# Attention and a two-layer feed-forward on one NeuronCore: three quarters of the first layer as seven products, and kv in 64-column tiles

## The chip, the core and the metric

The kernel runs on one core of a Trainium2 chip. The metric is the device time of one execution in microseconds (us). "TensorE" multiplies matrices into PSUM; VectorE (DVE in the profile), ScalarE (ACT) and GpSimd (POOL) work beside it; SyncE (SP), GpSimd and ScalarE issue DMAs. A 128x512 float32 result in PSUM is one bank in this text.

## The reference

```python
kv = einsum('bhsd,bhse->bhde', k, v)            # batch 8, 8 heads, sequence 576, head 64
o  = einsum('bhsd,bhde->bhse', q, kv)
o  = o / sqrt(mean(o*o, -1) + 1e-6) * g_norm
x  = o.transpose(0, 2, 1, 3).reshape(4608, 512)
h  = x @ w_in                                   # 512 x 2048
g  = h * sigmoid(1.702 * h)
out = g @ w_out                                 # 2048 x 512
```

All inputs and the output are float32; the kernel casts to float16 on the way in and accumulates in float32.

## The kernel before

The 4608 tokens are nine tiles of 512: tiles t = 0 to 7 hold the first 512 tokens of batch element t, and tile 8 the eight remainders of 64. A tile has two stages. The **hidden stage** forms h transposed, 16 columns of 128 hidden units by 512 tokens, each gated by ScalarE into `gT`. The **projection** multiplies `gT` by `w_out`. Attention for the next batch element is woven into both: kv of t+1 in the hidden stage, its q·kv rows, norms and the transpose of x in the projection. The order of each engine's instructions is the order in which the program issues them (a manual schedule). `dense` runs a tile, and the lists `u1` and `u2` (filled with `at1(step, ...)` and `at2(step, ...)`) say after which step of the hidden stage or of the projection an attention piece is issued.

From tile 2 on (`SEVEN`) part of the hidden stage, and from tile 1 on the whole projection, use Strassen's scheme in its Winograd form: a product of matrices cut into quarters takes seven products of quarters in place of eight, for sums of the inputs and outputs formed on VectorE.

- In the hidden stage (`hid_seven`), `PARTS = (2, 6)` names two groups, each of two column blocks and the two that lie `HF` = 8 blocks higher: eight of 16 columns. A product is four matmuls of 256 columns (`SevenIn.product`). The other eight columns are plain: four matmuls of 512 columns each, run as two halves. Products and halves alternate; a group's seven go in the order 1, 5, 6, 2, 7, 3, 4.
- Products 1, 6, 7 and 4 of a group accumulate one after the other in one PSUM bank (x), 5 and 3 in another (z), and 2 has its own (y). So what a product leaves has to be read before the next one writes into its bank: ScalarE copies 1 (L548) and 6 (L552), VectorE copies 5 (L550) and adds 2, 7 and 3 (L557), ScalarE gates the four results (L525).
- The sums of the weights are formed once (`w_in_sum`, L478), the sums of x once a tile (`Sums.form`, L492), the sums of `gT` (`Seven.sums`, L588) as its columns become ready.
- The projection (`Seven.run`, L656) is seven products of 16 matmuls of 256 columns.

kv of tiles 2 to 7: the rows of k and v are loaded 64 partitions a head, so that the two heads of a pair fill 128 (`load_half`, L112). VectorE packs k into `kpad`, each head in its own 64 of 128 columns beside zeros (`pack_k`, L224), and a pair of heads takes nine matmuls of 64 columns on the full array (`kv`, L233). The four pairs lie at four steps of the hidden stage. Four copies on VectorE (`keep_kv`, L249) place the results. The next loads of k wait for the packing, those of v for the kv matmuls. Batch element 0 is computed otherwise (`First`): 96 partitions, six rows each, and 64-column matmuls for each head (L393).

Of the kernel before, what the change touches and what calls it, by code (L numbers as in the profile page):

```python
# [7 lines left out]
F16 = mybir.dt.float16  # L8
# [4 lines left out]
P = 128  # L13
# [3 lines left out]
def kernel(  # L17
# [29 lines left out]
    PH = P // 2  # L47
    NH = S // PH
    assert PH == D and PH * NH == S

# [16 lines left out]
    kpad = const.tile([P, NPAIR, NH, P], F16)  # L67
# [15 lines left out]
    PARTS = (2, 6)  # L83
# [26 lines left out]
    def load_half(n, b, c0, c1):  # L110
        for l in range(2):
            nc.gpsimd.dma_start(  # L112
                out=raw[n][l * PH : (l + 1) * PH, c0:c1, 0 : NH * D],
                in_=srcs[n][b].rearrange("(c l) (p j) d -> l p c (j d)", l=2, j=NH)[l][:, c0:c1],
            )

    def load_kv(b):
        load_half("k", b, 0, NPAIR)
        load_half("v", b, 0, NPAIR)
# [86 lines left out]
    class Attention:  # L206
# [14 lines left out]
        def pack_k(self, c0=0, c1=NPAIR):  # L221
            for l in range(2):
                r = slice(l * PH, (l + 1) * PH)
                nc.vector.tensor_copy(  # L224
                    out=kpad[r, c0:c1, :, l * D : (l + 1) * D],
                    in_=kraw[r, c0:c1, 0 : NH * D].rearrange("p c (j d) -> p c j d", j=NH),
                )

        def kv(self, c):
            if c % self.KEEP == 0:  # L230
                self.kvp = ps_a.tile([P, NPAIR, D], F32, name="kvp", tag="att")
            for j in range(NH):
                nc.tensor.matmul(  # L233
                    self.kvp[:, c, :],
                    kpad[:, c, j, :],
                    vbuf[:, c, j * D : (j + 1) * D],
                    start=(j == 0),
                    stop=(j == NH - 1),
                )
            if (c + 1) % self.KEEP == 0:  # L240
                self.keep_kv(c + 1 - self.KEEP, c + 1)

        def keep_kv(self, c0, c1):
            kb = self.kb.rearrange("p (c l) e -> p c l e", l=2)
            for half in range(2):
                to = slice(half * D, (half + 1) * D)
                for hl in range(2):
                    r = slice(hl * D, (hl + 1) * D)
                    nc.vector.tensor_copy(kb[to, c0:c1, hl, to], self.kvp[r, c0:c1, :])  # L249
# [133 lines left out]
    class First(Early):  # L383
# [4 lines left out]
        def kv(self, c):  # L388
            t = ps_o.tile([P, D], F32, name="kv0", tag="o")
            for j in range(NJ):  # L390
                for hl in range(2):
                    x = slice((hl * NJ + j) * D, (hl * NJ + j + 1) * D)
                    nc.tensor.matmul(  # L393
                        t[hl * D : (hl + 1) * D, :],
                        kraw[0:PE_, c, x],
                        vbuf[0:PE_, c, x],
                        start=(j == 0),
                        stop=(j == NJ - 1),
                    )
# [66 lines left out]
    def w_in_sum(n):  # L466
        for g, i in enumerate(PARTS):
            a11, a12, a21, a22 = quarters(
                w_in_sb, slice(i * P, (i + 2) * P), slice(0, KH)
            )  # L470
            o = [ws[:, m, :, 2 * g * P : 2 * (g + 1) * P] for m in range(4)]
            op, a, b = (
                (nc.vector.tensor_add, a21, a22),
                (nc.vector.tensor_sub, o[0], a11),
                (nc.vector.tensor_sub, a11, a21),
                (nc.vector.tensor_sub, a12, o[1]),
            )[n]
            op(o[n], a, b)  # L478
# [15 lines left out]
    class SevenIn:  # L494


        ORDER = (1, 5, 6, 2, 7, 3, 4)

        def __init__(self, hid, xs, g):
# [4 lines left out]
            self.both = s12  # L504
# [24 lines left out]
        def product(self, p):  # L529
# [23 lines left out]
            elif p == 4:  # L553
                self.gate(1, 0, o)
            else:
                which, r, n = {2: ("s1", 0, 0), 7: ("s5", 1, 1), 3: ("s2", 0, 1)}[p]
                nc.vector.tensor_add(s[which], o, s[which])  # L557
                self.gate(r, n, s[which])
# [132 lines left out]
    def hid_seven(t, hid, seven, units1):  # L691

        pairs = [i for i in range(HF) if all(i not in (g, g + 1) for g in PARTS)]
        halves = [(f, k) for i in pairs for f in (i, HF + i) for k in (0, KH)]
        xs = xsums.pop(t)
        steps = [halves[0], halves[1]]
        for g in range(len(PARTS)):
            part = SevenIn(hid, xs, g)
            for n, p in enumerate(part.ORDER):
                steps += [(part, p), halves[2 + g * len(part.ORDER) + n]]  # L700
        for n, (f, k) in enumerate(steps):
            if isinstance(f, SevenIn):
                f.product(k)
            else:
                for ko in (k, k + 1):
                    hid.mm(ko, f)
                if k:
                    hid.gate(f)
            for u in units1.get(n, ()):
                u()  # L710
            which = {17: 0, 20: 1, 23: 2, 26: 3}.get(n)
            if which is not None:
                seven.sums(0, 4, (which,))
        seven.sums(4, 8, (0,))

    def dense(t, units1, units2, group, deep, hid=None):
# [52 lines left out]
        else:  # L769
            i = 4 if t >= SEVEN else 6  # L770
# [100 lines left out]
    load_half("k", 1, 0, 2)  # L871
    load_w_out(8, 10)
    load_w_out(10, 12)
    load_half("v", 1, 0, 2)
    load_half("k", 1, 2, NPAIR)
    load_half("v", 1, 2, NPAIR)
# [4 lines left out]
    SEVEN = 2  # L881
    HALVED = (2, 3, 4, 5, 6)
# [9 lines left out]
    for t in range(NT):  # L892
# [12 lines left out]
        if t == 0:  # L905
# [6 lines left out]
            for l in range(2):  # L912
                r = slice(l * PH, (l + 1) * PH)
                at1(8, nc.vector.memset, kpad[r, :, :, (1 - l) * D : (2 - l) * D], 0.0)
                at1(9, nc.vector.memset, kvd[l], 0.0)
            at1(13, load_q, 2)
            for c in range(NPAIR):
                at1(12, of(1, "pack_q", c))
                at2(9 + 3 * c, of(1, "q", c))
                if c % 2 == 0:  # L920
                    at2((21, 0, 38)[c], of(1, "pack_k", c, c + 2))
# [7 lines left out]
        elif b < B:  # L929
            if t == 1:  # L930
# [10 lines left out]
                for n, at in ((2, 82), (0, 86), (1, 92), (3, 97)):  # L941
                    at2(at, w_in_sum, n)
            f0 = 5 if t == 1 else 3
            late = 14 if t == 1 else 15
            if t == 1:
                at1(f0, start, b)
# [53 lines left out]
```

## Time and profile before

| | us |
|---|---|
| three executions | 275.87, 275.74, 274.12 (median 275.74) |
| the profiled execution | 274.47 |
| its span, first to last instruction | 272.7 |

In the profile's groups a row gives line, engine, operation, tiles and shapes, the count, then busy time in us and the mean in ns, then the idle time before and what ended it. In the timeline a row begins with start and duration in us; merged rows (x4) last from the first's start to the last's end. In the rows of stretches, each engine has its busy time and number of instructions, in the order PE, weight loads, DVE, ACT, POOL; then TensorE's granted clock, the DMA share and GB/s. A matmul's row lasts until its result is in PSUM; the next one starts long before.

### The profile page before, as it was taken

To read this page: it belongs to the slowest core of one execution; us is meant where nothing else is said; L and a number is where in the kernel's file an instruction comes from. 1 tells how busy PE (TensorE), PEld (TensorE's weight loads), DVE (VectorE), ACT (ScalarE), POOL (GpSimd) and SP (SyncE) were. 2 spreads that over 40 slices of the span, in tenths; PEclk is the share of its full clock that TensorE was granted. 3 is DMA by queue.
4 is the path that set the end of the run, shared out by engine and by line. 5 is a ranking of instruction groups with operands and counts; after the bars stand their busy time and mean duration, and the time that the engine had idled before them with its cause. 6 is when DMAs were issued, how large, how long until landed. Compare 5 with 4: busy or idle time off the path is not lost.

```text
span 272.7 us, 5717 instructions
## 1 busy us (share of the span) xinstructions
PE 263.0 (96%) x2328; PEld 189.3 (69%) x2328; DVE 184.7 (68%) x331; ACT 172.8 (63%) x309; POOL 50.3 (18%) x82
## 2 busy tenths in 40 slices
PE   7799999999999999999999999999999999999993
PEld 6344554458767787778777877788778867876782
DVE  1642454958998787779777976797689646455731
ACT  3578509858857865686577657775678477228610
POOL 8772363114014101410031003200000000000000
PEclk9999999999999999999999999999999999999999
DMA  8999999989989929993899289937500610021005
GB/s 175 182 199 204 205 203 199 270 161 155 132 161 166 141 46 185 180 164 31 185 174 181 33 177 170 189 36 170 153 0 2 155 77 2 0 99 58 0 2 154
DMA packets 56540, 35.29 MB, mean 129 GB/s; under 512 B 31810, under 2 KB 53826, under 8 KB 56386
## 3 DMA queue, kind: packets, MB, share of 16 engines
q0 software_dynamic: 25184, 17.91, 46.1%
q1 hardware_dynamic: 30848, 16.49, 26.3%
q10 hardware_dynamic: 482, 0.52, 0.6%
q8 instruction: 18, 0.29, 0.5%
q14 instruction: 8, 0.07, 0.1%
HBM read 36.70 MB, written 9.44 MB: 169 GB/s over the span
## 4 chain that ended last, share of the span: by engine, by line
PE 81%; DVE 7%; ACT 4%; DMA 3%; POOL 2%; issue 1%; DVEq 0%; ACTq 0%
PE o L656 30%; PE hT L449 26%; PE h L538 15%; PE o L750 4%; PE kvp L233 3%; DMA w_in_sb<-in_moe_w_in_dram 3%; PE outR L297 2%; DVE gS L588 2%; ACT gT L525 1%; DVE ws L478 1%; ACT gT L458 1%; PE ss L345 1%; DVE w_in_sb L204 1%; POOL qraw L93 1%; DVE x L325 1%
## 5 line engine op out<-in xcount | busy, mean ns | idle before, releaser
L449 PE MATMUL hT<-xT,w_in_sb 128*128 128x512 f16 x320 | 85.4, 379 | 1.3 <-DMA w_in_sb<-in_moe_w_in_dram 1.3
L458 ACT ACTIVATE gT<-hT 128x512 f16<-128x512 f32 x88 | 50.8, 601 | 12.5 <-PE hT L449 12.4
L656 PEld LDWEIGHTS <-gS 128*128 128x128 f16 x512 | 49.6, 98 | 6.7 <-DVE gS L588 0.9
L656 PE MATMUL o<-tw,gS 128*128 128x256 f16 x384 | 47.6, 273 | 0.3 <-DVE gS L588 0.3
L449 PEld LDWEIGHTS <-w_in_sb 128*128 128x128 f16 x352 | 32.5, 98 | 19.3 <-DMA w_in_sb<-in_moe_w_in_dram 1.6
L656 PEld LDWEIGHTS <-gT 128*128 128x128 f16 x384 | 37.0, 98 | 5.7
L525 ACT ACTIVATE gT<-qf 128x512 f16<-128x512 f32 x42 | 26.4, 629 | 18.7 <-DVE qf L557 18.5
L557 DVE TENSOR_TENSOR qf<-h,qf 128x512 f32<-128x512 f32 x42 | 28.3, 688 | 9.9 <-PE h L538 9.6
L656 PE MATMUL o<-w_out_sb,gT 128*128 128x256 f16 x256 | 33.7, 273 | 0.0
L538 PEld LDWEIGHTS <-ws 128*128 128x128 f16 x224 | 21.9, 98 | 14.8 <-issue 0.3
L588 DVE TENSOR_TENSOR gS<-gT 128x1024 f16<-128x1024 f16 (+1 forms) x34 | 22.3, 656 | 13.8 <-ACT gT L458 13.7
L112 POOL DMA_DIRECT2D kraw<-in_k_dram x16 | 9.9, 622 | 88.6 <-DVE kpad L224 82.6
L538 PE MATMUL h<-xS,ws 128*128 128x256 f16 x168 | 25.2, 272 | 0.1
L538 PEld LDWEIGHTS <-w_in_sb 128*128 128x128 f16 x168 | 16.4, 98 | 11.9 <-issue 1.9
L633 DVE TENSOR_TENSOR osb<-o,qf 128x512 f32<-128x512 f32 (+1 forms) x25 | 16.6, 665 | 11.6 <-issue 6.4
L347 ACT ACTIVATE ln<-ss,eps_t 128x512 f32<-128x512 f32 (+1 forms) x16 | 9.3, 582 | 15.0 <-PE ss L345 14.9
L625 ACT COPY qf<-o 128x512 f32<-128x512 f32 (+1 forms) x26 | 14.5, 560 | 5.4 <-PE o L656 5.4
L750 PE MATMUL o<-w_out_sb,gT 128*128 128x512 f16 x64 | 16.7, 379 | 0.0
L325 DVE TENSOR_TENSOR x<-outR,sum 128x512 f16<-128x512 f32 x24 | 14.9, 684 | 1.0 <-ACT sum L321 1.0
L900 ACT ACT_TABLE_LOAD x12 | 15.4, 1283 | 0.2
L656 PE MATMUL o<-w_out_sb,gS 128*128 128x256 f16 x128 | 15.4, 273 | 0.0
L656 PE MATMUL o<-tw,gT 128*128 128x256 f16 x128 | 15.3, 272 | 0.0
(97 smaller groups left out, 348.1 us busy)
## 6 DMA issues: line engine op xcount, KB each, us to landing
out_dram<-osb SPq DMA_DIRECT2D x10, 512.0 KB, 3.0
kraw<-in_k_dram POOLq DMA_DIRECT2D x12, 288.0 KB, 6.3
vbuf<-in_v_dram POOLq DMA_DIRECT2D x12, 288.0 KB, 7.4
qraw<-in_q_dram POOLq DMA_DIRECT2D x3, 512.0 KB, 9.0
qbuf<-in_q_dram POOLq DMA_DIRECT2D x3, 512.0 KB, 9.7
out_dram<-osb SPq DMA_DIRECT2D x6, 192.0 KB, 5.2
w_in_sb<-in_moe_w_in_dram POOLq DMA_DIRECT2D x4, 256.0 KB, 7.9
w_out_sb<-in_moe_w_out_dram POOLq DMA_DIRECT2D x2, 512.0 KB, 13.9
```

The source lines that it names most:

```text
L325: nc.vector.tensor_mul(self.x16[:, j0 : j0 + 2, c0 : c0 + DM // 2].rearrange("p l (h d) -> p h l d", d=D), self.o[j][0].rearrange("p (h l ...
L449: nc.tensor.matmul(self.h[fo], w_in_sb[:, ko, fo * P : (fo + 1) * P], self.x[:, ko], start=(ko == 0), stop=(ko == KO - 1),)
L458: nc.scalar.activation(self.gT[:, fo, :], self.h[fo], AFT.Gelu_apprx_sigmoid)
L525: nc.scalar.activation(self.gT[:, to, n * TH : (n + 1) * TH], src, AFT.Gelu_apprx_sigmoid)
L538: nc.tensor.matmul(o[:, a], w, x, start=(p in (1, 2, 5) and a == 0 and k == 0), stop=(k == KH - 1), skip_group_check=True,)
L557: nc.vector.tensor_add(s[which], o, s[which])
L588: op(s[:, n, lo], a, b)
L625: nc.scalar.copy(self.kept[as_][:, m], ps)
L633: nc.vector.tensor_add(o, ps, self.kept[with_][:, m])
L656: nc.tensor.matmul(o, a, w, start=(p in (1, 2, 5) and i == 0 and (mo == 0 or split)), stop=(i == HF - 1), skip_group_check=True,)
L750: nc.tensor.matmul(os[mo], gT[:, fo, mo * P : (mo + 1) * P], w_out_sb[:, fo, :], start=(fo == 0), stop=(fo == FO - 1),)
L900: u2.setdefault(i, []).append(lambda: f(*args))
```

## The change

- `PARTS` becomes `(0, 3, 6)`: three groups, twelve of 16 columns as seven products (84 matmuls of 256 columns in place of 56), and four plain columns (16 matmuls of 512 in place of 32). Each group has its own copies, adds and gates, which makes 12 in place of 8 weight sums.
- The order of the steps is a list, `STEPS`. A group's products go 1, 2, 5, 6, 3, 7, 4, and the next group's 1 and 2 are placed between 7 and 4. Gates are issued one step later than what they gate. Between products 5 and 3, and between 7 and 4, two other steps now lie (in the second group kv stands between 5 and 3 as well).
- `READY` issues the sums of `gT` for columns 0 to 2 after steps 15, 18, 20 and 21, those for columns 3 and 4 after steps 24, 26, 28 and 29, and the first for columns 5 to 7 at the end. Before, they covered columns 0 to 3 and 4 to 7.
- kv runs as one block at the step "kv" (15), after step 11 in tile 1: for each of four pairs, six times two matmuls in 64-column tiles from 96 partitions, reading k as it was loaded. `kpad`, `pack_k`, `load_half` and the zeroing of `kpad` go. k and v are loaded in one DMA each, and both loads wait for kv's matmuls. Two of the four copies of kv go to ScalarE.
- Two of the four weight sums (`w_in_sum` 3 and 2, six instructions on VectorE) move from the projection of tile 1 to the first step of tile 2.

```diff
-    PARTS = (2, 6)
+    PARTS = (0, 3, 6)
...
     def load_kv(b):
-        load_half("k", b, 0, NPAIR)
-        load_half("v", b, 0, NPAIR)
+        early_load("k", b, 0, NPAIR)
+        early_load("v", b, 0, NPAIR)
...
+        def kv_product(self, t, c):
+            for j in range(NJ):
+                for hl in range(2):
+                    x = slice((hl * NJ + j) * D, (hl * NJ + j + 1) * D)
+                    nc.tensor.matmul(
+                        t[hl * D : (hl + 1) * D, :],
+                        kraw[0:PE_, c, x],
+                        vbuf[0:PE_, c, x],
+                        start=(j == 0),
+                        stop=(j == NJ - 1),
+                    )
...
-                    nc.vector.tensor_copy(kb[to, c0:c1, hl, to], self.kvp[r, c0:c1, :])
+                    copy = nc.scalar.copy if half else nc.vector.tensor_copy
+                    copy(kb[to, c0:c1, hl, to], self.kvp[r, c0:c1, :])
...
-                self.gate(1, 0, o)
+                return lambda: self.gate(1, 0, o)
...
-                self.gate(r, n, s[which])
+                return lambda: self.gate(r, n, s[which])
...
+        parts = [SevenIn(hid, xs, g) for g in range(len(PARTS))]
+        gates = []
+        for n, step in enumerate(STEPS):
+            behind, gates = gates, []
+            if step == "h":
+                f, k = next(halves)
                 for ko in (k, k + 1):
                     hid.mm(ko, f)
                 if k:
-                    hid.gate(f)
+                    gates.append(lambda f=f: hid.gate(f))
+            elif step != "kv":
+                g, p = step
+                gate = parts[g].product(p)
+                if gate:
+                    gates.append(gate)
+            for u in behind:
+                u()
             for u in units1.get(n, ()):
                 u()
-            which = {17: 0, 20: 1, 23: 2, 26: 3}.get(n)
-            if which is not None:
-                seven.sums(0, 4, (which,))
-        seven.sums(4, 8, (0,))
+            for i0, i1, which in READY.get(n, ()):
+                seven.sums(i0, i1, which)
+        for u in gates:
+            u()
+        seven.sums(5, 8, (0,))
...
+    STEPS = [(0, 1), (0, 2), "h", "h", (0, 5), (0, 6), "h", (0, 3), (0, 7), (1, 1), (1, 2), (0, 4)]
+    STEPS += ["h", (1, 5), (1, 6), "kv", (1, 3), (1, 7), (2, 1), (2, 2), (1, 4)]
+    STEPS += ["h", (2, 5), (2, 6), "h", (2, 3), (2, 7), "h", "h", (2, 4)]
+    KV = STEPS.index("kv")
+    READY = {n: [(0, 3, (w,))] for w, n in enumerate((15, 18, 20, 21))}
+    READY |= {n: [(3, 5, (w,))] for w, n in enumerate((24, 26, 28, 29))}
...
-                for n, at in ((2, 82), (0, 86), (1, 92), (3, 97)):
-                    at2(at, w_in_sum, n)
+                at2(82, w_in_sum, 0)
+                at2(90, w_in_sum, 1)
+            if t == 2:
+                at1(0, w_in_sum, 3)
+                at1(0, w_in_sum, 2)
...
-            at1(f0, of(b, "pack_k"))
-            for c in range(NPAIR):
-                at1(10 + c if t == 1 else 8 + 2 * c, of(b, "kv", c))
+            at1(late, of(b, "kv_all"))
```

More of the change, by code (lines that the diff above doesn't have):

```diff
@@ L219, in __init__ @@
                 self.x16 = attn.tile([P, J, DM], F16, name="x16", tag="x16", bufs=1)
[L221 to L227, printed above, removed]
         def kv(self, c):
@@ L389, in kv @@
             t = ps_o.tile([P, D], F32, name="kv0", tag="o")
[L390 to L399, printed above, removed]
+            self.kv_product(t, c)
             nc.vector.tensor_mul(
```

76 lines of the change are left out of this document (24 added, 52 removed).

## The prediction

> **What bounds the kernel now.** I read the page's shares first, then the stretches of one tile (its hidden stage, then its projection), then the timeline where TensorE pauses.
>
> ```profile
> span 272.7 us, 5717 instructions
> PE 263.0 (96%) x2328; PEld 189.3 (69%) x2328; DVE 184.7 (68%) x331; ACT 172.8 (63%) x309; POOL 50.3 (18%) x82
> ...
> 76.64:91.55 14.91, 14.57 (x127) 9.57 (x125) 13.59 (x26) 9.60 (x18) 4.63 (x7) 1.00 0.98 181
> ...
> 133.30:147.39 14.09, 14.07 (x125) 9.55 (x123) 11.96 (x22) 9.71 (x18) 4.62 (x7) 1.00 1.10 194
> ...
> 216.63:229.71 13.08, 13.08 (x90) 8.61 (x88) 8.17 (x14) 9.55 (x18) 0.00 (x0) 1.00 0.21 82
> ```
>
> TensorE is busy 96% of the span; in the hidden stage of tile 4 it is busy 14.07 of 14.09 us at full clock (1.00). That tile's first matmul is at 133.14 (below), so its stage is 14.25 us. But VectorE is busy 11.96 us of it and ScalarE 9.71, with 8.17 and 9.55 where there is no kv (tile 7). So TensorE bounds the kernel, and the other two are near enough to take over.
>
> ```profile
> 50.81 5.99 PE L449 MATMUL hT<-xT,w_in_sb 128*128 128x512 f16 x27
> ...
> 116.77 0.60 PE L538 MATMUL h<-xS,ws 128*128 128x256 f16 x4
> ...
> 117.95 1.28 DVE L557 TENSOR_TENSOR qf<-h,qf 128x512 f32<-128x512 f32 x2
> ...
> 118.69 0.60 PE L538 MATMUL h<-xS,w_in_sb 128*128 128x256 f16 x4
> ...
> 122.75 3.00 PE L656 MATMUL o<-tw,gS 128*128 128x256 f16 x26
> ...
> 133.14 1.03 PE L449 MATMUL hT<-xT,w_in_sb 128*128 128x512 f16 x4
> ```
>
> The only pause of such a stage is here: product 4 of the second group waits for the add that reads product 7 from the same PSUM bank. The first add runs 117.95 to 118.64, and TensorE goes on at 118.69, 0.05 later. A 512-column matmul costs (5.99-0.38)/26 = 0.216 us, a 256-column one (3.00-0.27)/25 = 0.109; a product (four) 0.436, a plain half (two) 0.432.
>
> **What TensorE saves.** Per tile from 2 to 8, 16 plain matmuls go (3.46 us) and 28 product matmuls come (3.05): -0.41.
>
> ```profile
> 7.25 0.38 PE L393 MATMUL kv<-vbuf,kraw 96*64 96x64 f16 x12
> ...
> 112.60 0.42 PE L233 MATMUL kvp<-vbuf,kpad 128*128 128x64 f16 x9
> 112.86 0.60 PE L449 MATMUL hT<-xT,w_in_sb 128*128 128x512 f16 x2
> ...
> 125.68 0.31 PE L268 MATMUL outT<-qTr,kvd 64*64 64x64 f16 x8
> 125.92 0.28 PE L656 MATMUL o<-tw,gS 128*128 128x256 f16 x1
> ```
>
> Now a pair's nine kv matmuls push the next matmul back 0.26, a tile's 1.04. The new kv is 48 matmuls in 64-column tiles. The row of 12 (six pairs) gives (0.38-0.20)/5.5 = 0.03 us for two. The 64x64 row shows the change of mode: the last matmul before it starts at 122.75+2.73 = 125.48, so the way in takes 0.20 instead of 0.11, and the way out 0.12. 24 pairs at 0.032 and both ways: 0.98, so -0.06 a tile. Bounds: 0.7 (no change of mode) to 1.3 (0.38 for each 12, less the tail). Tile 0's four separate kv pay the change each time: 0.09 in, 0.18 for twelve, 0.12 out, 0.39 against 0.26 now, +0.45 in all with rounding.
>
> [...]
>
> If nothing else changed, seven tiles would save 0.41 and six kv 0.06: -3.2 us.
>
> **What VectorE and ScalarE take on.** Mean durations by group (ns, after the bar), then rows of the timeline:
>
> ```profile
> L557 DVE TENSOR_TENSOR qf<-h,qf 128x512 f32<-128x512 f32 x42 | 28.3, 688 | 9.9 <-PE h L538 9.6
> L525 ACT ACTIVATE gT<-qf 128x512 f16<-128x512 f32 x42 | 26.4, 629 | 18.7 <-DVE qf L557 18.5
> ...
> L588 DVE TENSOR_TENSOR gS<-gT 128x1024 f16<-128x1024 f16 x30 | 20.6, 688 | 13.8 <-ACT gT L458 13.7
> ...
> L550 DVE COPY qf<-h 128x512 f32<-128x512 f32 x14 | 9.7, 692 | 3.9 <-PE h L538 3.5
> ...
> L552 ACT COPY qf<-h 128x512 f32<-128x512 f32 x14 | 8.2, 584 | 3.6 <-PE h L538 3.6
> ...
> L588 DVE TENSOR_TENSOR gS<-gT 128x512 f16<-128x512 f16 x4 | 1.7, 420 | 0.0
> ```
>
> ```profile
> 109.90 0.60 PE L538 MATMUL h<-xS,ws 128*128 128x256 f16 x4
> ...
> 110.60 0.69 DVE L557 TENSOR_TENSOR qf<-h,qf 128x512 f32<-128x512 f32 x1 [0.43 <-PE h L538]
> ...
> 113.07 1.73 DVE L249 CAST kvd<-kvp 64x256 f16<-64x256 f32 x4 [0.70 <-PE kvp L233]
> ...
> 115.03 0.60 PE L538 MATMUL h<-xS,ws 128*128 128x256 f16 x4
> ...
> 115.67 0.59 ACT L552 COPY qf<-h 128x512 f32<-128x512 f32 x1 [0.65 <-PE h L538]
> ...
> 121.17 1.10 ACT L305 ACTIVATE sq<-outR 128x512 f16<-128x512 f32 x2
> ```
>
> A product begun at 115.03 is copied from 115.67, one begun at 109.90 is added from 110.60: a result is taken 0.20 (copies) to 0.27 us after TensorE has moved on. In a queue the next instruction starts about 0.1 before the last one's end (two adds 1.28, two activations 1.10), so an add holds VectorE 0.60 and an activation ScalarE 0.48 to 0.53. The kv copies hold VectorE 0.43 each. A sum over three columns (768) lies between the 512 and 1024 rows: 0.555 (0.46 held), an estimate.
>
> The third group adds three adds and a copy on VectorE, two copies and the gating of four half-width results on ScalarE. Gone are packing k (two copies) and two of four kv copies from VectorE; the two go to ScalarE (estimate 0.38 each). By throughput both still fit into the stage. By order they do not. In the new order two steps (0.87 us) lie between products 5 and 3, and two between 7 and 4; the copy or add between needs 0.20+0.69+0.05 = 0.94 at once, and 0.12 to 0.8 more if something is queued in front. I therefore follow tile 4 by hand through the compiled order of the three queues (each instruction starts when its queue is free and its inputs are there), from the first matmul at 0. (g,p) is product p of group g; "3.11 for 3.04" is when TensorE can start that product, and when it would have without this wait. The input sums are done by 1.2:
>
> (0,3): copy of (0,5) 2.37 to 3.06, TensorE at 3.11 for 3.04. (0,7): ScalarE gates (0,2) and a plain column first, copies (0,6) 3.00 to 3.58; 3.63 for 3.55. (0,4): adds of (0,3) at 3.75, of (0,7) 4.35 to 5.04; 5.09 for 4.94. kv ends at 7.81. (1,7): ScalarE copies (1,1) to 5.59, VectorE adds (1,2) to 6.32, ScalarE then has three gates (6.36, 6.89, 7.37) ahead of the copy of (1,6), 7.84 to 8.43; 8.48 for 8.25. (1,4): VectorE has two kv copies from 7.92, a sum at 8.78, the add of (1,3) at 9.24 and then that of (1,7), 9.84 to 10.52; 10.57 for 9.78. (2,3): gate (1,3) 9.96, copy (2,1) to 11.08, add (2,2) 11.12, two sums, copy (2,5) 12.76 to 13.45; 13.50 for 12.75. (2,4): adds at 14.14 and 14.74 to 15.42; 15.47 for 15.24.
>
> The stage ends at 15.91 for 14.25: 2.31 us of waits, of which 1.5 are (1,4) and (2,3). Tiles 3 to 6: +1.65 each, +6.6. Tiles 7 and 8 have no kv; the same steps end at 15.15 for 13.08. A wait of 0.33 in their projection goes, as the last sums are now shorter:
>
> ```profile
> 231.46 0.60 PE L656 MATMUL o<-tw,gS 128*128 128x256 f16 x4
> 232.22 0.50 PE L656 MATMUL o<-tw,gS 128*128 128x256 f16 x3 [0.16 <-DVE gS L588]
> ```
>
> (232.22 follows 231.46+0.33 by 0.43 for 0.11.) So +1.75 each, +3.5. Tile 2 also gets six of the twelve weight sums (L478) after its first product, ahead of its first add:
>
> ```profile
> 74.85 1.42 DVE L478 TENSOR_TENSOR ws<-w_in_sb 128x512 f16<-128x512 f16 x4
> ...
> 76.64 0.81 PE L449 MATMUL hT<-xT,w_in_sb 128*128 128x512 f16 x3
> ...
> 77.46 0.76 DVE L478 TENSOR_TENSOR ws<-w_in_sb,ws 128x512 f16<-128x512 f16 x2
> 78.12 0.42 DVE L492 TENSOR_TENSOR xS<-xT 128x512 f16<-128x512 f16 x1
> ...
> 79.26 0.42 DVE L492 TENSOR_TENSOR xS<-xT,xS 128x512 f16<-128x512 f16 x1
> ```
>
> Its input sums, now where the two weight sums at 77.46 stood, end queueing at 78.93 (four in 1.14+0.33). Six weight sums at (1.42-0.42)/3 = 0.33 follow, so the first add starts at 80.94, 4.3 after the tile's start for 1.26. The copy of (0,5) then lets (0,3) go at 5.64, and (0,4) at 8.09 for 5.09. Its stage is 18.9 for 14.91: +4.0.
>
> Loads: k's (POOL) now waits for kv, as v's does, some 5 us later; one instruction replaces two. Its next use is a tile away. Nothing taken, bounds 0 to +1 a tile (rival below). Tile 1's kv: -0.06.
>
> Sum: 0.45 - 0.06 + 4.0 + 6.6 + 3.5 = +14.5 us on the profiled execution's 274.47 (span 272.7): 289.0. That execution is 1.3 below the median of 275.74.
>
> **Rivals.** (a) The interlocking hides the waits: -3.2, and the present pause of 0.19 and the 0.33 go: 270 to 272, faster. For it: VectorE's work fits the stage by throughput. It decides if the 2.6 us between the end of kv and the end of (1,7)'s add shrink under the 1.74 of four products. Against it: five measured durations in one queue. (b) Only waits with an idle queue remain: 0.07 at two places, 0.12 at three, 0.5 a tile, which the savings of 0.41, 0.06 and 0.19 cancel: 273 to 275, no difference. (c) Queues cost half of that, because an order or lag is a little kinder than followed: 278 to 283. (d) The later k load runs into the transposes of x.
>
> ```profile
> 107.85 1.40 POOL L112 DMA_DIRECT2D kraw<-in_k_dram  x2 [18.42 <-DVE kpad L224]
> ...
> 113.33 1.22 POOL L112 DMA_DIRECT2D vbuf<-in_v_dram  x2 [4.07 <-PE kvp L233]
> ...
> 133.16 0.42 DVE L492 TENSOR_TENSOR xS<-xT 128x512 f16<-128x512 f16 x1 [0.88 <-DMA xT<-x]
> ```
>
> k is asked for at 107.85 now, v at 113.33; afterwards both when kv ends. x of tile 4 lands at its very start already (133.16, first matmul 133.14); a delay of 1 us at three or four tiles gives 292. (e) The two column tiles do not run side by side in the crowded stage: 48 single steps of 0.03 (0.26/9) and both ways make a kv 1.6 instead of 0.98, 293. [...]
>
> **How the numbers follow.** The forecast 0.55 (own range 284 to 292, from the bounds of kv and of the estimated rows), (c) 0.19, (d) 0.06, (e) 0.02, (a) 0.10, (b) 0.08. The likeliest is 289.0; from 279 to 293 about 8 in 10 lie: most of (c), (d) and the forecast; (a) and (b) are left out. About 1% (2.7 us) is what a measurement can tell: faster 0.10 from (a), within 0.08 from (b), slower 0.82 from the rest.
>
> **What would show it.** Right: TensorE waits before the second group's product 4 for the add of product 7 and before the third's product 3 for the copy of product 5, 0.7 each; tile 2's product 3 waits over 2 us; stages near 15.9, 18.9 and 15.2 us; 48 kv matmuls in 0.8. Wrong: stages at or under 14 us with VectorE taking results at once, tiles starting late for xT, or a kv over 1.5 us.

## The result, and the profile after

| | before | after |
|---|---|---|
| median of four executions, us | 275.71 (274.12 to 275.87) | 290.60 (289.42 to 292.78) |
| the profiled execution | 274.47 | 291.39 |
| its span | 272.7 | 289.6 |

The ratio is 1.0563, with a 95% interval of 1.0484 to 1.0642: 5.6% slower. The first view is the profile's page of the kernel after (span, busy times by engine, TensorE's granted clock in 40 slices).

```profile
span 289.6 us, 6131 instructions
PE 267.4 (92%) x2496; PEld 196.7 (68%) x2496; DVE 189.4 (65%) x361; ACT 185.1 (64%) x335; POOL 42.2 (15%) x66
...
PEclk9999999999979999999999999999999999999999
```

TensorE's share falls from 96% to 92% although it has more instructions, and no other engine is near its limit: the time went into waits. One slice of the clock reads 7, at tile 2. The next lines are stretches of the same trace: the hidden stages of tiles 2 (from when TensorE is free for it), 4 and 7, and a piece of tile 2.

```profile
77.06:97.61 20.55, 16.23 (x150) 11.33 (x148) 15.69 (x33) 12.19 (x23) 3.69 (x5) 0.92 0.55 105
...
141.22:157.31 16.09, 14.60 (x150) 10.49 (x148) 12.05 (x23) 11.98 (x23) 3.68 (x5) 1.00 0.85 169
...
230.34:245.48 15.14, 13.69 (x103) 9.73 (x101) 11.28 (x21) 11.15 (x21) 0.00 (x0) 1.00 0.17 70
83.85:87.26 3.41, 3.41 (x17) 2.35 (x16) 1.91 (x3) 1.87 (x4) 0.00 (x0) 0.50 0.00 0
```

The stages last 20.55, 16.09 and 15.14 us for 14.91, 14.25 and 13.08. VectorE's busy time in tile 4's stage is as before (12.05 for 12.10 from its first matmul), ScalarE's 11.98 for 9.71. The last row is new: 3.41 us at a granted clock of 0.50.

Tile 4's timeline after, with the two long waits (151.91 and 154.84) and what they wait for:

```profile
148.22 0.95 PE L222 MATMUL kvp<-vbuf,kraw 96*64 96x64 f16 x48
...
149.10 0.61 PE L522 MATMUL h<-xT,ws 128*128 128x256 f16 x4
...
149.99 0.54 DVE L572 TENSOR_TENSOR gS<-gT 128x768 f16<-128x768 f16 x1
...
150.30 0.93 PE L522 MATMUL h<-xT,w_in_sb 128*128 128x256 f16 x7
...
150.56 1.29 DVE L541 TENSOR_TENSOR qf<-h,qf 128x512 f32<-128x512 f32 x2
...
151.91 0.60 PE L522 MATMUL h<-xS,w_in_sb 128*128 128x256 f16 x4 [0.68 <-DVE qf L541]
...
153.63 0.55 DVE L572 TENSOR_TENSOR gS<-gT,gS 128x768 f16<-128x768 f16 x1
153.64 0.59 PE L432 MATMUL hT<-xT,w_in_sb 128*128 128x512 f16 x2
...
154.10 0.68 DVE L534 COPY qf<-h 128x512 f32<-128x512 f32 x1
...
154.84 0.60 PE L522 MATMUL h<-xT,ws 128*128 128x256 f16 x4 [0.60 <-DVE qf L534]
```

How such a wait is read: of the seven matmuls from 150.30 the last starts at 150.30+0.93-0.27 = 150.96, so the next could start at 151.07; it starts at 151.91, 0.84 late, and 0.06 after the two adds that begin at 150.56 end (151.85). The sum at 149.99 is queued in front of these. In the same way 153.64+0.59-0.38+0.22 = 154.07, and 154.84 is 0.76 late, behind VectorE's copy, which itself stood behind a gate sum of 0.55. Step by step in tile 4, in us:

| (group, product) | (0,3) | (0,7) | (0,4) | (1,7) | (1,4) | (2,3) | (2,4) | sum |
|---|---|---|---|---|---|---|---|---|
| foretold | 0.07 | 0.08 | 0.15 | 0.23 | 0.79 | 0.75 | 0.24 | 2.31 |
| measured | 0.08 | 0.12 | 0.19 | 0.21 | 0.84 | 0.76 | 0.31 | 2.51 |

And by stage, each from its first matmul to that of the next (tile 2's from when TensorE is free for it):

| stretch | before | after | change | foretold |
|---|---|---|---|---|
| start to tile 2 | 76.64 | 77.06 | +0.42 | +0.39 |
| tile 2, hidden stage | 14.91 | 20.55 | +5.64 | +4.0 |
| tiles 3 to 6, hidden stages | 57.03 | 64.85 | +7.82 | +6.6 |
| tiles 7 and 8, hidden stages | 26.16 | 30.27 | +4.1 | +4.1 |
| projections and the end | | | -1.1 | -0.7 |
| span | 272.7 | 289.6 | +16.9 | +14.5 |

Tile 2's timeline after shows where the largest difference lies:

```profile
77.25 0.58 ACT L620 COPY osb<-o 128x512 f32<-128x512 f32 x1 [1.16 <-PE o L640]
...
77.89 1.03 PE L522 MATMUL h<-xT,w_in_sb 128*128 128x256 f16 x8 [0.67 <-ACT osb L620]
...
79.33 1.08 DVE L465 TENSOR_TENSOR ws<-w_in_sb,ws 128x512 f16<-128x512 f16 x3
...
80.34 1.09 DVE L465 TENSOR_TENSOR ws<-w_in_sb 128x512 f16<-128x512 f16 x3
...
81.35 0.68 DVE L541 TENSOR_TENSOR qf<-h,qf 128x512 f32<-128x512 f32 x1
81.95 0.68 DVE L534 COPY qf<-h 128x512 f32<-128x512 f32 x1
...
82.68 0.60 PE L522 MATMUL h<-xT,ws 128*128 128x256 f16 x4 [1.59 <-DVE qf L534]
```

The tile now begins with a product, whose bank ScalarE has still to empty from the projection (77.25): 0.84 that the prediction did not have. It cost nothing, since the six weight sums keep the first add until 81.35 either way; the wait at 82.68 is 0.84 shorter for it. All waits of the stage (0.84, 1.75, 0.59, 1.05, 0.76, 0.31) make 5.30 beside 13.59 of work, 18.89, which is the 18.9 foretold. The other 1.66 is the half clock: 3.41 us in which a 256-column matmul takes 0.213 for 0.109. The four executions bear this out: their mean granted clocks were 1.000, 0.997, 0.992 and 0.986, their spans 287.6, 288.0, 289.6 and 291.0.

### The profile page after: what moved, and what is told of

Its sections match the earlier page's. It is cut to its first block, busy times and chain, and to the rows that moved or that the text cites. A ratio compares the mean times of both kernels' runs of the same rounds, so it can differ in the third digit from the quotient of the medians.

```text
span 289.6 us, 6131 instructions
## 1 busy us (share of the span) xinstructions
PE 267.4 (92%) x2496; PEld 196.7 (68%) x2496; DVE 189.4 (65%) x361; ACT 185.1 (64%) x335; POOL 42.2 (15%) x66
## 4 chain that ended last, share of the span: by engine, by line
PE 63%; DVE 18%; ACT 9%; DMA 3%; issue 3%; POOL 2%; DVEq 0%
PE o L640 28%; PE hT L432 13%; PE h L522 12%; DVE qf L541 7%; PE o L739 4%; DVE gS L572 3%; ACT gT L509 3%; DMA w_in_sb<-in_moe_w_in_dram 2%; PE kvp L222 2%; ACT qf L532 2%; PE outR L289 2%; DVE qf L534 1%; DVE ws L465 1%; DMA xT<-x 1%; DVE xS L479 1%
## 5 line engine op out<-in xcount | busy, mean ns | idle before, releaser
L509 ACT ACTIVATE gT<-qf 128x512 f16<-128x512 f32 x63 | 39.5, 631 | 27.4 <-DVE qf L541 27.4
L432 PE MATMUL hT<-xT,w_in_sb 128*128 128x512 f16 x224 | 55.6, 380 | 1.0 <-DMA w_in_sb<-in_moe_w_in_dram 1.0
L541 DVE TENSOR_TENSOR qf<-h,qf 128x512 f32<-128x512 f32 x63 | 41.8, 688 | 18.7 <-PE h L522 8.5
L522 PEld LDWEIGHTS <-ws 128*128 128x128 f16 x336 | 32.4, 98 | 23.5 <-issue 13.3
L441 ACT ACTIVATE gT<-hT 128x512 f16<-128x512 f32 x60 | 33.9, 602 | 3.7 <-PE hT L432 3.6
L572 DVE TENSOR_TENSOR gS<-gT 128x768 f16<-128x768 f16 (+2 forms) x48 | 24.3, 505 | 6.8 <-ACT gT L441 6.8
L522 PE MATMUL h<-xT,w_in_sb 128*128 128x256 f16 x144 | 19.5, 281 | 0.7 <-ACT osb L620 0.7
L317 DVE TENSOR_TENSOR x<-outR,sum 128x512 f16<-128x512 f32 x24 | 14.9, 682 | 4.8 <-ACT sum L313 4.8
L303 DVE TENSOR_REDUCE sum<-sq 128x8 f32<-128x512 f16 x24 | 16.0, 682 | 3.2 <-ACT sq L297 2.6
L522 PE MATMUL h<-xS,w_in_sb 128*128 128x256 f16 x84 | 13.0, 278 | 5.2 <-DVE qf L541 4.2
L534 DVE COPY qf<-h 128x512 f32<-128x512 f32 x21 | 14.4, 687 | 4.9 <-PE h L522 4.9
## 6 DMA issues: line engine op xcount, KB each, us to landing
w_out_sb<-in_moe_w_out_dram POOLq DMA_DIRECT2D x2, 512.0 KB, 13.8
```

The costliest lines, as they stand in the source:

```text
L303: nc.vector.tensor_reduce(out=self.sum4[:, j, :], in_=self.o[j][1].rearrange("p (x d) -> p x d", d=D), op=ALU.add, axis=mybir.AxisListType.X,)
L317: nc.vector.tensor_mul(self.x16[:, j0 : j0 + 2, c0 : c0 + DM // 2].rearrange("p l (h d) -> p h l d", d=D), self.o[j][0].rearrange("p (h l ...
L432: nc.tensor.matmul(self.h[fo], w_in_sb[:, ko, fo * P : (fo + 1) * P], self.x[:, ko], start=(ko == 0), stop=(ko == KO - 1),)
L441: nc.scalar.activation(self.gT[:, fo, :], self.h[fo], AFT.Gelu_apprx_sigmoid)
L509: nc.scalar.activation(self.gT[:, to, n * TH : (n + 1) * TH], src, AFT.Gelu_apprx_sigmoid)
L522: nc.tensor.matmul(o[:, a], w, x, start=(p in (1, 2, 5) and a == 0 and k == 0), stop=(k == KH - 1), skip_group_check=True,)
```

## The experiments

Each is compared with runs of the kernel before on the same chip (medians 274.1 to 274.2). The table gives tile 4 in each, in us, from the first matmul of a stage to the first of the next:

| kernel | hidden stage | projection | tile |
|---|---|---|---|
| before | 14.25 | 13.58 | 27.83 |
| after | 16.09 | 13.58 | 29.67 |
| kv alone, copies on both engines | 14.76 | 13.58 | 28.33 |
| kv alone, copies on VectorE | 14.52 | 13.58 | 28.10 |
| gate sums late | 15.15 | 15.53 | 30.68 |
| gate sums late, before the turns | 15.15 | 13.67 | 28.82 |
| steps spaced | 14.59 | 15.64 | 30.23 |
| steps spaced, 2 | 14.31 | 14.09 | 28.40 |
| steps spaced, 4 | 13.64 | 14.73 | 28.37 |

**The new kv alone, in the kernel before.** One block after step 15, two of the four copies on ScalarE, as in the change.

```diff
-            at1(f0, of(b, "pack_k"))
-            for c in range(NPAIR):
-                at1(10 + c if t == 1 else 8 + 2 * c, of(b, "kv", c))
+            at1(late, of(b, "kv_all"))
```

> The kernel before with the new kv alone: 64-column tiles from 96 rows, no packing, one block after step 15, two of its copies on ScalarE; the two groups and their order stay. If the queues of VectorE and ScalarE make the loss (the theory), kv itself is nearly free: 0.06 saved in six tiles, 0.45 lost in tile 0, the 0.19 pauses perhaps gone, so 0.994 to 1.002 of the kernel before. If the 64-column tiles cost much in the stage (rival: weight loads or changes of mode), 1.02 or more.

Measured: 277.61 us, ratio 1.0135 [1.0094, 1.0175]; neither number was met. The timeline of this kernel in tile 3:

```profile
114.11 0.95 PE L231 MATMUL kvp<-vbuf,kraw 96*64 96x64 f16 x48
...
115.10 0.86 DVE L250 CAST kvd<-kvp 64x256 f16<-64x256 f32 x2 [1.49 <-PE kvp L231]
...
116.05 0.74 ACT L250 CAST kvd<-kvp 64x256 f16<-64x256 f32 x2 [0.80 <-PE hT L450]
...
116.81 0.58 ACT L549 COPY qf<-h 128x512 f32<-128x512 f32 x1
...
117.45 0.60 PE L539 MATMUL h<-xS,ws 128*128 128x256 f16 x4 [0.55 <-ACT qf L549]
```

The kv matmuls are as cheap as foretold. But ScalarE's two copies start only at 116.05, after VectorE's second has ended (115.96), and ScalarE's copy of product 1 (L549), whose bank product 6 needs, is queued behind them: TensorE waits 0.71 in each of five tiles. VectorE's work in tile 4's stage had fallen to 9.1 us from 12.1, and the stage was longer all the same: the order decides, not the load. Part of the median is the clock: the two executions at clocks of 0.998 and 1.000 took 276.77 and 276.87.

**The same, with all four copies on VectorE.**

```diff
-                    copy = nc.scalar.copy if half else nc.vector.tensor_copy
-                    copy(kb[to, c0:c1, hl, to], self.kvp[r, c0:c1, :])
+                    nc.vector.tensor_copy(kb[to, c0:c1, hl, to], self.kvp[r, c0:c1, :])
```

> The kernel before with the new kv alone, all four kv copies on VectorE (in the first such run two of them stood on ScalarE). Theory: that run's 0.71 us a tile were ScalarE's two kv copies, which started only after VectorE's two and held the copy of product 6 behind them. Without them that wait is gone, the kv costs what the matmul rows say, and the packed copies saved on VectorE hide the rest: ratio to before 0.995 to 1.004 (273 to 275 us). Rival (the 48 small matmuls or the later load cost it): the ratio stays at 1.010 to 1.018.

Measured: 275.44 us, 1.0048 [1.0032, 1.0065], just above the range. The 0.71 is gone, so it was ScalarE's queue. What stays is the old pause before the second group's product 4, now 0.52 for 0.19: the four copies lie in one piece in VectorE's queue ahead of its add. Removing two packing copies thus gained nothing.

**The weight sums back in tile 1's projection, in the kernel after.**

```diff
+                for n, at in ((2, 82), (0, 86), (1, 92), (3, 97)):
+                    at2(at, w_in_sum, n)
-                at2(82, w_in_sum, 0)
-                at2(90, w_in_sum, 1)
-            if t == 2:
-                at1(0, w_in_sum, 3)
-                at1(0, w_in_sum, 2)
```

> The changed kernel with all four weight sums in the projection of tile 1, at the places of the kernel before (three instructions each now). Theory: tile 2 no longer waits 1.75 and 0.59 us for its first copies, and its clock does not fall, so 3 to 4 us less than the changed kernel: 286 to 288, ratio 1.040 to 1.047. If tile 2's loss has another cause, 290 as now.

Measured: 290.18 us, 1.0588 [1.0573, 1.0604], a miss. The sums still stood ahead of tile 2's work in the same queue. The wait at (0,3) fell from 1.75 to 0.99, but product 5 now waited 0.73 for the input sums: the stage took 18.97, for the 18.89 that the kernel after takes without its half clock. The tile also began 0.55 later, but the sums are not the cause: tile 1's projection took 15.47 for 15.46, and the 0.55 was already there at the end of tile 0's hidden stage (29.59 for 29.05).

**Gate sums out of the hidden stage, in the kernel after.** Only the first of the four sums of `gT` stays there; the third and fourth follow at steps 40 and 50 of the projection.

```diff
-    READY = {n: [(0, 3, (w,))] for w, n in enumerate((15, 18, 20, 21))}
-    READY |= {n: [(3, 5, (w,))] for w, n in enumerate((24, 26, 28, 29))}
+    READY = {26: [(0, 5, (0,))]}
...
+                later = {6: [lambda: seven.sums(0, 8, (1,))]}
+                later |= {40: [lambda: seven.sums(0, 8, (2,))], 50: [lambda: seven.sums(0, 8, (3,))]}
```

> The changed kernel with the sums of the gated values taken out of the hidden stage: one instruction for columns 0 to 4 after step 26 instead of eight, the other three sums in the projection. Theory: fewer instructions stand in VectorE's queue ahead of the adds and copies; the wait before the second group's product 4 falls from 0.84 to about 0.35, that before the third group's product 3 from 0.76 to about 0.1, 1.0 us a tile, seven tiles: 283 to 284.5, ratio 1.027 to 1.035. If only the distance of the steps counts and not the queue, 290 as now.

Measured: 293.49 us, 1.0709 [1.0693, 1.0725]. In the hidden stage (1,4) went from 0.84 to 0.37 and (2,3) from 0.76 to 0.08 as expected, with 0.44 new at (2,7) behind a ScalarE copy; the stage fell by 0.94, but the time went up. The timeline of this kernel's projection of tile 3:

```profile
132.11 2.48 DVE L317 TENSOR_TENSOR x<-outR,sum 128x512 f16<-128x512 f32 x4 [1.23 <-ACT sum L313]
...
134.51 1.22 DVE L572 TENSOR_TENSOR gS<-gT 128x2048 f16<-128x2048 f16 x1
...
135.78 0.94 PE L640 MATMUL o<-tw,gS 128*128 128x256 f16 x7 [1.77 <-DVE gS L572]
```

The sum was issued behind the four "turns" (L317: VectorE multiplies the q·kv rows by their norm factors), which wait 1.23 for ScalarE's roots. VectorE stands idle with the sum's inputs long ready, and TensorE's product 7 starts 1.94 late.

**The same, the third sum at step 30, ahead of the turns.**

```diff
-                later |= {40: [lambda: seven.sums(0, 8, (2,))], 50: [lambda: seven.sums(0, 8, (3,))]}
+                later |= {30: [lambda: seven.sums(0, 8, (2,))], 50: [lambda: seven.sums(0, 8, (3,))]}
```

> The changed kernel with the gate sums out of the hidden stage, as in the run before, but the third of them asked for at step 30 of the projection, ahead of the four turns that wait for ScalarE, and the fourth at step 50 behind them. Theory (what counts is the place in VectorE's queue): the 1.94 us a tile at product 7 of the projection goes to under 0.2, the hidden stage keeps its 0.37 and 0.08 in place of 0.84 and 0.76, and the time is 281 to 284 us, 6 to 9 under the changed kernel. Rival (VectorE has no room left in the projection wherever the sums stand): a wait of over 1 us a tile stays, 286 to 291.

Measured: 284.54 us, 1.0396 [1.0362, 1.0431], 0.5 above the expected end, 6.1 under the kernel after. The 1.94 fell to 0.08. So some 40% of the change's loss was gate sums that stood in front of adds and copies. This run also tells something of the clock. Tile 2 had the pauses of the kernel after (1.75 and 0.59), yet in its timeline the eight matmuls behind them run at the full rate (1.04 for eight) and the stage's granted clock was 1.00:

```profile
82.49 0.60 PE L522 MATMUL h<-xT,ws 128*128 128x256 f16 x4 [1.59 <-DVE qf L534]
...
83.51 0.60 PE L522 MATMUL h<-xS,ws 128*128 128x256 f16 x4 [0.43 <-ACT qf L536]
...
83.95 1.04 PE L522 MATMUL h<-xT,w_in_sb 128*128 128x256 f16 x8
```

**Steps spaced.** kv first in the tile, and at least three steps between most products and the one that needs their bank or result; weight sums and gate sums as in the second and third runs above; bank y from the pool of the plain columns. In `ORDER`, A, B and C are the three groups, each with the product's number, and h is a plain half.

```diff
+    ORDER = "kv h A1 h A5 h A6 B1 A2 B5 A7 B6 A3 B2 A4 B7 h B3 C1 C5 B4 C6 h C2 h C7 h C3 h C4"
+    STEPS = [("ABC".index(w[0]), int(w[1])) if w[0] in "ABC" else w for w in ORDER.split()]
+    READY = {27: [(0, 5, (0,))]}
```

> Same products, plain columns and kv, in another order: kv first, the three groups interleaved so that three steps lie wherever a product writes over what another engine still reads, bank y in the plain columns' pool; sums of gated values as in e3, weight sums as in e2. Theory: the waits are a matter of order; with them gone, a tile's hidden stage is 13.7 to 14.2 us and the time 272 to 277, ratio 0.99 to 1.005. Rival (three groups are too much work for ScalarE and VectorE whatever the order): stages above 15 us, 283 or more.

Measured: 290.92 us, 1.0625 [1.0599, 1.065]. The time is in the rival's range, the stage in neither: it fell to 14.59. The 1.96 behind the turns is that of the late gate sums, and tile 2 had pauses of 1.02 and 2.47 and then a half clock (the twelfth of the page's 40 slices, 79.5 to 86.7 us, reads 8).

**Spaced, 2.** All kv copies on VectorE, the third group's bank x from the attention pool, the third gate sum at step 30.

```diff
+                if (self.g, name) == (2, "x"):
+                    pool, tag = ps_a, "att"
...
-                later |= {40: [lambda: seven.sums(0, 8, (2,))], 50: [lambda: seven.sums(0, 8, (3,))]}
+                later |= {30: [lambda: seven.sums(0, 8, (2,))], 50: [lambda: seven.sums(0, 8, (3,))]}
```

> The changed kernel with its steps in another order (kv first; at least three steps between a product whose result is taken and the product that needs that bank or result), all four kv copies on VectorE, the third group's shared bank from the other pool, the weight sums in the tile before, and the gate sums placed as in the run beside it. Theory: a hidden stage of tiles 3 to 6 then waits under 0.3 us in all and lasts 13.7 to 13.9 for 14.25 before; with tile 2 still 2 to 4 us late behind the weight sums the time is 273 to 277. Rival (VectorE and ScalarE are too full for any order): the waits move and still sum to over 1 us a tile, 280 or more.

Measured: 278.61 us, 1.0169 [1.0154, 1.0184]. Neither range was met, and the rival's condition of over 1 us a tile was: two waits stay, 0.41 at product 3 of the projection (its gate sum is behind the turns) and 0.77 at the third group's product 6. The timeline of tile 3 shows the second:

```profile
116.01 0.58 ACT L508 ACTIVATE gT<-h 128x512 f16<-128x512 f32 x1
...
116.49 0.62 ACT L508 ACTIVATE gT<-qf 128x512 f16<-128x512 f32 x1
...
117.01 0.59 ACT L440 ACTIVATE gT<-hT 128x512 f16<-128x512 f32 x1
...
117.49 0.59 ACT L533 COPY qf<-h 128x512 f32<-128x512 f32 x1
...
118.12 0.49 PE L523 MATMUL h<-xS,ws 128*128 128x256 f16 x3 [0.61 <-ACT qf L533]
```

Three gates in a row are ahead of the copy that TensorE waits for.

**Spaced, 4.** Both waits attacked: C1 two steps earlier, one plain half before C6, and the fourth gate sum ahead of the last turn.

```diff
-    ORDER = "kv h A1 h A5 h A6 B1 A2 B5 A7 B6 A3 B2 A4 B7 h B3 C1 C5 B4 C6 h C2 h C7 h C3 h C4"
+    ORDER = "kv h A1 h A5 h A6 B1 A2 B5 A7 B6 A3 B2 A4 B7 C1 B3 C5 B4 h C6 h C2 h C7 h C3 h C4"
...
-                later |= {30: [lambda: seven.sums(0, 8, (2,))], 50: [lambda: seven.sums(0, 8, (3,))]}
+                later |= {30: [lambda: seven.sums(0, 8, (2,))], 36: [lambda: seven.sums(0, 8, (3,))]}
```

> The kernel of the 278.6 us run with two moves. Its trace leaves two waits in each tile: 0.774 us at the third group's product 6, which waits for ScalarE's copy of product 1 (queued behind three gates), and 0.411 at product 3 of the projection, which waits for the fourth gate sum behind the turns. Product 1 of the third group goes two steps earlier and one plain half between it and product 6 (0.87 us more distance), and the fourth gate sum goes ahead of the last turn. Theory (order and distance are all that is left): both waits go, 1.18 us in each of five tiles and 0.77 in tiles 7 and 8, 7.4 us together: 271 to 272.5, ratio 0.988 to 0.994. Rival (the queues are full, so another wait takes their place): 275 to 278.

Measured: 277.18 us, 1.0131 [1.0099, 1.0162], the rival's range. Both waits are gone, and the hidden stage is what the prediction's arithmetic of TensorE gives without waits. Stretches of tile 4, the kernel before and this one:

```profile
133.14:147.39 14.25, 14.23 (x126) 9.65 (x125) 12.10 (x22) 9.71 (x18) 4.62 (x7) 1.00 1.10 197
147.39:160.97 13.58, 13.58 (x139) 12.07 (x138) 10.18 (x18) 9.45 (x18) 0.00 (x0) 1.00 0.64 86
```

```profile
135.99:149.63 13.64, 13.64 (x149) 10.61 (x149) 10.07 (x19) 10.77 (x20) 3.68 (x5) 1.00 1.21 210
149.63:164.36 14.73, 13.83 (x139) 11.96 (x137) 12.80 (x21) 9.39 (x17) 0.00 (x0) 1.00 0.50 76
```

The stage gives 0.61, the projection takes 1.15. In it VectorE runs without a gap (timeline of tile 3's projection; each row starts before the one ahead ends), and TensorE, which would have started L336 at 130.69, waits 1.06 for the bank that the last turn reads:

```profile
125.78 1.27 DVE L302 TENSOR_REDUCE sum<-sq 128x8 f32<-128x512 f16 x2
...
126.96 1.21 DVE L573 TENSOR_TENSOR gS<-gT 128x2048 f16<-128x2048 f16 x1
...
128.09 1.88 DVE L316 TENSOR_TENSOR x<-outR,sum 128x512 f16<-128x512 f32 x3
...
129.89 1.21 DVE L573 TENSOR_TENSOR gS<-gT,gS 128x2048 f16<-128x2048 f16 x1
...
131.02 0.68 DVE L316 TENSOR_TENSOR x<-outR,sum 128x512 f16<-128x512 f32 x1
...
131.76 0.27 PE L336 MATMUL ss<-sq,ones 128*128 128x256 f16 x1 [0.90 <-DVE x L316]
```

Here my theory that order and distance are all falls: with the fourth sum behind the last turn TensorE waited for the sum (spaced, 2), with the sum ahead it waits for the turn. For the whole tile TensorE's busy time fell by 0.34 (27.81 to 27.47), VectorE's rose by 0.59 (22.28 to 22.87) and ScalarE's by 1.00 (19.16 to 20.16).

**Weight scaling first in tile 1's projection** ("spaced, 2" and all four scalings of `w_in` by `g_norm` on VectorE at step 0, the weight sums at steps 30, 50, 58 and 66).

```diff
-                at2(48, scale_w_in, 1, nc.scalar)
-                at2(58, scale_w_in, 0, nc.vector)
-                at2(65, scale_w_in, 2, nc.vector)
-                at2(72, scale_w_in, 3, nc.vector)
-                for n, at in ((2, 82), (0, 86), (1, 92), (3, 97)):
+                for ko in (0, 2, 1, 3):
+                    at2(0, scale_w_in, ko, nc.vector)
+                for n, at in ((2, 30), (0, 50), (1, 58), (3, 66)):
```

> As the kernel beside it, and the scaling of the first layer's weights moved to the start of tile 1's projection on VectorE, the twelve weight sums spread over the same projection. Theory: tile 2's delay is only the place of this work in VectorE's queue, so most of its 2 to 4 us goes and the time is 270 to 273, ratio to before 0.985 to 0.997. Rival (the work is late wherever it stands, or it delays the normalisation of tile 2): the time is that of the kernel beside it or more, 274 to 278.

Measured: 281.41 us, 1.0274 [1.0239, 1.0309], above both ranges. Tile 2 then had no wait at its input sums, but the delay had moved: the sums stood ahead of the turns, TensorE waited 2.5 us for the turns in tile 1's projection, and then the clock was at a half for 3.4 us (the eleventh of the page's 40 slices, 69.6 to 76.6 us, reads 7).

**Two scalings at step 30** (in "spaced, 4").

```diff
-                at2(58, scale_w_in, 0, nc.vector)
-                at2(65, scale_w_in, 2, nc.vector)
-                at2(72, scale_w_in, 3, nc.vector)
+                at2(30, scale_w_in, 0, nc.vector)
+                at2(30, scale_w_in, 2, nc.vector)
+                at2(65, scale_w_in, 3, nc.vector)
```

> As the kernel beside it, and two of the three weight scalings on VectorE at step 30 of tile 1's projection, where VectorE stands idle about 1.1 us before the turns, for steps 58 and 65. Theory (tile 2's 1.01 at the input sums is the length of VectorE's queue ahead of it): that wait falls by about 1.0 and the 0.92 behind it too, the turns start 0.25 later: 0.7 to 1.7 us under the kernel beside it, 269.5 to 271.5. Rival (as in the run with all four scalings ahead, the turns' delay returns as a TensorE wait before the last rows): the time is that of the kernel beside it or up to 1 us more.

Measured: 277.52 us, 1.0123 [1.0107, 1.0139], the rival's number; tile 2's waits of 1.01 and 0.92 did not move. The weight sums still stood at step 82, behind instructions that need ScalarE and TensorE, and VectorE was idle for 1.27 us in front of them.

**Six of the weight sums at steps 66 and 70 too.**

```diff
-                for n, at in ((2, 82), (0, 86), (1, 92), (3, 97)):
+                for n, at in ((2, 66), (0, 70), (1, 92), (3, 97)):
```

> As the 277.5 us kernel with two scalings ahead, and six of the twelve weight sums asked for at steps 66 and 70 of tile 1's projection for 82 and 86. In that kernel VectorE stands idle from 73.0 to 74.3 and from 74.6 to 75.5 while the sums wait behind instructions that need ScalarE and TensorE, which is why moving the scalings alone changed nothing (1.01 stayed 1.01). Theory (place in the queue): five or six sums of 0.335 move into these holes, tile 2's 1.01 and 0.92 fall to under 0.4 together: 1.0 to 1.6 us less, 275.9 to 276.6, while tiles 3 to 6 keep their 1.06. Rival: the sums delay the last rows' work and TensorE waits there instead, 277 to 278.5.

Measured: 277.04 us, 1.0098 [1.0069, 1.0127]. That is in the rival's range, and with executions from 276.43 to 279.15 the 0.5 less than in the run before is not sure. The trace shows both: tile 2's stage goes from 15.55 to 13.78, as the theory has it, for 0.42 more in tile 1's projection, as the rival has it.

**The third gate sum on GpSimd** (as the run before, with this sum asked for at step 9 and the fourth back at step 50).

```diff
-                    (nc.vector.tensor_sub, g[:, lo, r1], g[:, lo, r2]),
+                    ((nc.gpsimd if self.t >= SEVEN else nc.vector).tensor_sub, g[:, lo, r1], g[:, lo, r2]),
...
-                later |= {30: [lambda: seven.sums(0, 8, (2,))], 36: [lambda: seven.sums(0, 8, (3,))]}
+                later |= {9: [lambda: seven.sums(0, 8, (2,))], 50: [lambda: seven.sums(0, 8, (3,))]}
```

> As the kernel beside it, and the third gate sum of tiles 2 to 8 on GpSimd, which is 16% busy; the fourth goes back behind the turns. In the kernels with no wait left in the hidden stage TensorE waits 1.06 us a tile in the projection for VectorE's last turn. Theory (VectorE's queue between the hidden stage and the turns, full to the end, is the bound there): 1.13 us off that queue let the turns start about 0.9 earlier, the 1.06 falls under 0.2, five tiles give 4.3 to 5.3 us: 270.5 to 272.5, ratio under 1. Rival (GpSimd takes the sum late, over 6 us, or slows VectorE's own instructions while it runs): a wait of over 1 us at the sixth product's successor in the projection, or longer VectorE instructions, 276 or more.

Measured: 295.65 us, 1.0794 [1.0757, 1.083]. The timeline of tile 3 in this kernel:

```profile
123.32 4.05 POOL L573 TENSOR_TENSOR gS<-gT 128x2048 f16<-128x2048 f16 x1 [9.49 <-ACT gT L508]
...
123.69 4.09 DVE L573 TENSOR_TENSOR gS<-gT 128x768 f16<-128x768 f16 x1 [0.45 <-ACT gT L440]
...
127.84 1.37 PE L641 MATMUL o<-tw,gS 128*128 128x256 f16 x11 [2.01 <-DVE gS L573]
```

The sum takes GpSimd 4.05 us for VectorE's 1.21, in time for product 7. But VectorE's own sum of 768 columns, 0.55 in the kernel after, lasts until 0.41 after GpSimd's end, and TensorE waits 2.2 for it. Over the run GpSimd's seven sums take 4.05 in the mean, and TensorE's idle time in front of the products that read these sums, put down to VectorE's, adds up to 17.6. That is the rival's longer VectorE instruction: 4.09 for 0.55 while GpSimd's sum runs.

## Why the prediction was right

- **TensorE's saving** was right: 13.59 of work foretold for a hidden stage, 13.64 measured once nothing waits (spaced, 4).
- **kv** was right: the next plain matmul, at 149.10, starts 0.97 later than it would without the block (0.88 from the block's first matmul at 148.22, way out included, and 0.09 for the way in ahead of it), for 0.98 foretold. Rival (e), one step after the other, is excluded: two matmuls start every 0.032 us (48 in 0.95, one lasting 0.20: 0.75 for 23.5 steps). Tile 0's price was too low, and summed wrongly: four times 0.13 is 0.52 and not 0.45, and its projection took 0.60 more (17.98 to 18.58). That the start to tile 2 still came out at +0.42 for +0.39 is luck, as the first hidden matmul came 0.18 earlier in this execution.
- **The waits of tiles 3 to 6** were right place by place in tile 4, 2.31 foretold and 2.51 measured; in tile 3 (2,4) waits 0.68 (0.31 in tile 4), and the four tiles cost 1.2 more than foretold. That order makes such waits is shown by runs that move one thing: moving only the gate sums took (1,4) from 0.84 to 0.37, and moving one sum ahead of the turns took 1.94 to 0.08. Spacing took all but 0.1 of the hidden stage's waits away, but together with other banks, kv's copies on VectorE and fewer sums in the stage, so its share alone is not shown.
- **Tiles 7 and 8** were right in length: 15.15 foretold, 15.14 measured; the 0.33 in tile 7's projection went as said. The prediction names no waits for them, and without kv they lie elsewhere than in tile 4: 0.51 before (1,3), 0.69 before (1,7), 0.07 before (1,4).
- **Tile 2** had its waits right (18.9) and its clock not thought of: 1.66 us in the profiled execution, up to 3.4 by the spread of the four spans. At a clock of 1.000 the kernel took 289.42, for 289.0 foretold; that it is so near is partly luck, as tiles 3 to 6 took 1.2 more than foretold, and the projections and the end 0.4 less.
- **ScalarE's kv copies** were priced at 0.38 each, an estimate, and nothing else; they take 0.363 to 0.367 in the kernel after. Alone in the kernel before, their place behind VectorE's copies cost 0.71 a tile. In the kernel after, the copy that this delays is not one that TensorE waits for there: the wait at (1,7) came out at 0.21 for 0.23.
- **Rivals.** (a) and (b) needed the waits hidden: the runs show that a spaced order hides those of the hidden stage, but gives 1.06 back in the projection. (c), half of the waits, is excluded by the 2.51. (d) did not happen: tile 4's first matmul follows the projection without a pause.

Open stays what would lift the last 1.06. Whether a fourth bank would do it, in the pool of three from which both the last turn's input and L336's result come, was not tried. No version here beats the kernel before.

## What to carry to other kernels

Fewer TensorE cycles bought with more work on the engines that read its results pay only if those queues have room at that place: follow each queue in its compiled order, with the 0.20 to 0.27 us of pick-up read from the profile before and the length of whatever stands in front, and the waits come out within some 10% (2.31 for 2.51 here). A wait taken away in one stage lets TensorE run ahead into the next, so price the whole loop's period: here the stage gained 0.61 and the projection gave back 1.15. An instruction that waits for another engine blocks everything issued behind it (1.94 a tile behind the turns, 0.71 behind the kv copies), so work whose inputs are ready belongs ahead of it.

## What was not expected of the hardware

- TensorE's granted clock fell to 0.50 from 83.85 to 87.26, for 3.41 us, after pauses of 1.75 and 0.59, and it stayed at 1.00 after equal pauses in another run ("gate sums late, before the turns"). One thing that differs is how the pauses lie in a grid of 3.41 us. The other fall in the trace of the kernel after, behind its last matmul, starts at 288.65, which is 204.80 after the first, or 60 steps of 3.413; in the other run the grid is counted back from the fall behind its last matmul, at 279.81. The stretch ahead of the fall in the kernel after, and the two stretches that hold the same pauses in the other run:

```profile
80.43:83.84 3.41, 1.40 (x11) 0.76 (x9) 2.35 (x6) 1.59 (x3) 0.00 (x0) 1.00 0.71 204
```

```profile
78.43:81.84 3.41, 2.47 (x17) 1.49 (x16) 3.41 (x11) 0.49 (x1) 0.00 (x0) 1.00 0.76 202
81.84:85.25 3.41, 2.33 (x20) 1.87 (x20) 1.94 (x3) 2.62 (x6) 0.00 (x0) 1.00 0.32 106
```

  In the first trace both pauses lie in one stretch, and TensorE is busy 1.40 us of it; in the second the longer pause lies across a step of the grid, and the two stretches hold 2.47 and 2.33. In the traces of the kernels before and after the only falls are this one and one in each behind the last matmul, after a whole stretch without TensorE (0.00); all their other whole stretches hold 1.76 us or more of busy TensorE, and none of them was followed by a fall. That the place of such pauses in the grid decides whether they cost 1.66 us is my reading of the two unlike outcomes; no run moves the pauses alone. Falls early in two other runs stay open: the third of the page's 40 slices, about 13.8 to 20.8 us, reads 7 with kv alone and copies on both engines, and 5 with six weight sums at steps 66 and 70.
- While GpSimd's sum of 4.05 us ran, VectorE's took 4.09 for 0.55 and ended 0.41 after it (tile 3 of the last run). What holds it up is not shown.
